# A tensor-product message kernel on one core: the product of the gathered rows gets a tile of its own

## The chip, the cores and the metric

The kernel runs on one core of one Trainium2 chip. The metric is the device time of the whole launch in microseconds (us). Five engines have instruction streams of their own: TensorE (PE), VectorE (DVE), ScalarE (ACT), GpSimd (POOL) and SyncE (SP). They wait for one another through semaphores. In the profile, "PE" is the matmul stream and "PEld" the loading of matmul weights; a "q" behind an engine's name (PEldq, DVEq) is its sequencer, which executes waits as small instructions of their own.

## The reference

There are N = 10,000 nodes with a feature block of 64 channels x 4 components (256 float32, 1 KB a row), and E = 640,000 edges, each with a source, a destination, four harmonics and four edge features.

```python
R   = silu(edge_feat @ w_rad)                        # (E, 64)
xs  = x[src]                                         # (E, 64, 4)
tp  = einsum('eci,ef,ifo->eco', xs, Y, cg)           # (E, 64, 4)
msg = R[:, :, None] * tp
agg = segment_sum(msg.reshape(-1, 256), dst, N).reshape(N, 64, 4)
out = einsum('ncm,cd->ndm', agg, w_mix)
```

So for each edge a row of x is gathered by its source, multiplied by a radial factor per channel, multiplied with the four harmonics, and summed into its destination node. The kernel sums x[src] * R * Y per destination first and applies `cg` and `w_mix` together to the sums (`wf` in the code).

## The kernel before

**Sort and messages.** The edges come in no order, so the kernel sorts them by destination in two passes (`pass1`, `pass2`), and the sorted edges then go through `messages()`. The edge list is cut into three parts (`SPLIT`, 32%, 37% and 31% of the edges), so that the sort of a later part runs while the messages of an earlier one are computed. The first 0.7 ms are sort alone; from then to about 10.06 ms the work of messages and the work of sort stand side by side on every engine; a short tail takes the few edges that did not fit.

**Units.** `messages()` goes through 939 units, 313 for each part. A unit is one block of 32 destination nodes, with its edges in tiles of 128: 5 tiles a unit in the first part (stage 1 here, 0.74 to 3.71 ms), 6 tiles in the second (stage 2, 3.72 to 7.03 ms). In the third (stage 3, 7.04 to 10.06 ms) units go in pairs: the even one has 6 tiles, the odd one 5, and the last tile of the even one may hold edges of both, so the odd unit's sums read it too. There are 156 such shared tiles. Stages 2 and 3 add to running sums that the stage before left in HBM (`old`, fetched by SP).

**What a unit does**, with the lines of the profile:
- gather (POOL, L1028): one indirect DMA for each tile fetches 128 rows of x into the unit's tile `xg`, [128, 6, 256] float32, of which there are `LG + 2` = 7 buffers.
- turn (PE, L1041), turned (ACT, L1046), radial (PE, L1053/1054), silu (ACT, L1057): the radial factors R of the unit come into `pre` in PSUM.
- spots (DVE, L1064, L1067): S, which says per edge which of the 32 nodes it goes to, times its harmonics. For a shared tile L1072 and L1074 make a second one, `Sx`, for the odd unit.
- products (DVE, L1081): R times the gathered rows, written over them: `xg` is operand and output. For a shared tile, `VX` keeps the view of it for the next unit's sums.
- sums (PE, L1094): per tile two matmuls of the product with S (in the trace each shows as two records), added up in `G`, one PSUM tile of which the even and the odd units take one half each. An odd unit with a shared tile has two more (`Sx`).
- evict (ACT, L1119, in stage 1; DVE, L1117, after that): G goes to `Gp` (stages 1 and 2, written back to HBM by SP, L1121) or `Gs` (stage 3). Every fourth unit of stage 3 the 128 nodes in `Gs` are multiplied with `wf` (PE, L1136) and stored.

**The order.** PE, DVE and ACT execute in the order in which the program is written (a manual schedule); what they do for other units is laid out by offsets in `quarters`: in step k the program writes, in four quarters with pieces of the sort between them,

```python
((index, LI), (gather, LG), (fetch, 2), (turn, 2), (sums, 0), (silu, 1), ...),
((turned, 2), (spots, 1)),
((products, 1), (evict, -1), ...), ((radial, 2), (full, -1))
```

The number is how many units ahead of k the piece works. So DVE does the product of unit k+1 and right behind it, in the same quarter, the eviction of unit k-1; the sums of unit k stand two quarters earlier in the program. Since both halves of `G` are one tile, the eviction of unit k-1 waits until the sums of unit k have been written. POOL and SP are not in the manual schedule: the order of their DMAs is chosen by a scheduler when the kernel is built, and waits follow from which buffer is free.

Of the kernel before, what the change touches and what calls it, by code (L numbers as in the profile page):

```python
# [18 lines left out]
F = mybir.dt.float32  # L19
BF = mybir.dt.bfloat16  # L20
I32 = mybir.dt.int32
OP = mybir.AluOpType
# [3 lines left out]
P = 128  # L26
# [10 lines left out]
PT = 2 * BT - 1  # L37
UT = 6
SPLIT = ((0.32, 5), (0.37, 6), (0.31, 6))
LG = 5  # L40
LI = 8
HEAVY = 4
BIG = 16384.0
# [36 lines left out]
class Kernel:  # L80
# [853 lines left out]
    def messages(self):  # L934

        nc, ph = self.nc, self.ph
# [3 lines left out]
        IDX, XG, PRE, ST_, RT, SS, VS, GP, GS, OLD, E9, ER, SX, VX = ({} for _ in range(14))  # L940
# [14 lines left out]
        def tiles(k):  # L955
            return place(*units[k])

        def shared(k):

            g, j = units[k]  # L960
            return g[0] == FIN and j % 2 == 0 and j + 1 < self.nb(g[1])
# [36 lines left out]
        def piece(q):  # L998
            def cast(k):

                at = block(k)
                if at is None:
                    return
                key, v, n = at
                if q == 0:
                    E9[key] = ph.tile([P, HB * MT, 3, 3, 4], BF, name="e9", bufs=2)
                    ER[key] = ph.tile([P, HB * MT, 4], F, name="er", bufs=1)
                r = ER[key][:, :n] if q else v
                nc.scalar.activation(E9[key][:, :n, :, q, :], r.unsqueeze(2).to_broadcast([P, n, 3, 4]), AF.Copy)
            return cast  # L1010
# [11 lines left out]
        def gather(k):  # L1022
            g, j = units[k]
            si, (t0, ut) = IDX[g][0], tiles(k)
            xg = XG[k] = ph.tile([P, UT, 256], F, name="xg", bufs=LG + 2)
            for t in range(ut):
                u = t0 + t
                nc.gpsimd.indirect_dma_start(  # L1028
                    out=xg[:, t, :], out_offset=None, in_=self.x,
                    in_offset=bass.IndirectOffsetOnAxis(ap=si[:, u:u + 1], axis=0))  # L1030
# [45 lines left out]

        def products(k):
            ut = tiles(k)[1]
            V = VS[k] = XG.pop(k)[:, :ut].rearrange("p t (c i) -> p t c i", i=4)
            R = RT.pop(k).rearrange("p (t c) -> p t c", c=64)  # L1080
            nc.vector.tensor_tensor(V, V, R.unsqueeze(3).to_broadcast([P, ut, 64, 4]), op=OP.mult)  # L1081
            if shared(k):
                VX[k + 1] = V[:, ut - 1]

        def sums(k):
            ut = tiles(k)[1]
            G = GP[units[k]] = Gb[:, k % 2]
            V, S = VS.pop(k), SS.pop(k)
            terms = [(V[:, t], S[:, t]) for t in range(ut)]
            if k in VX:  # L1090
# [49 lines left out]
        def mixed(k, po):  # L1140
# [5 lines left out]
        Gb = self.ps.tile([P, 2, 2, NB, 4], F, name="G", tag="G", bufs=1)  # L1146

        quarters = (((index, LI), (gather, LG), (fetch, 2), (turn, 2), (sums, 0), (silu, 1), (piece(0), 5), (piece(1), 4),
                     (piece(2), 3)), ((turned, 2), (spots, 1)),
                    ((products, 1), (evict, -1), (rest(0), 5), (rest(1), 4)), ((radial, 2), (full, -1)))  # L1150
        todo, po = [], None
        for k in range(-LI, n + 3):
# [434 lines left out]
```

## Time and profile before

| | |
|---|---|
| time, three runs | 10113.3, 10104.97, 10112.53 us; median 10112.53 |
| the profiled execution | 10113.46 us, its span 10111.7 us, mean granted PE clock 0.798 |
| busy share of the span | PE 65%, PEld 52%, DVE 71%, ACT 45%, POOL 58% |
| the 16 DMA engines | queue 0, which holds the gathers: 732.64 MB, 25.6% of their time; queue 1: 10.0% |
| gathers | 5165 indirect DMAs, POOL busy 955 ns for each |
| products | 939 instructions, 1516.9 us busy |
| sums | 20,660 records, 3256.9 us busy, and 624 for `Sx`, 125.7 us |

No engine is busy for the whole span. A row of the groups reads: line, engine, operation, output<-input, shapes, count | busy us and mean ns of one | idle time of the engine just before these instructions and what ended most of it. "issue" is time in which the engine waited for nothing that the profile shows, and "remote" is a release that the profile can't tie to an instruction of this core's records. Matmul ends are modelled.

### The profile page before, as it was taken

What the parts mean: (1) busy time and instruction counts of PE and PEld (TensorE: products, weight loads), DVE (VectorE), ACT (ScalarE), POOL (GpSimd) and SP (SyncE); (2) the same over time, 40 slices, a digit from 0 to 9 for tenths busy, and PEclk for the clock granted to TensorE, in tenths of its full rate; (3) what the DMA queues carried; (4) which work ended last, traced back from release to release, by engine and by line L of the source; (5) the groups of instructions that cost most, each with busy time, mean ns of one, the idle gap of its engine ahead of it and who ended that gap; (6) DMA issues with size and microseconds to landing.
All of it is one profiled execution on the core that took longest, in us unless ns stands there. A gap on an engine that the chain in (4) does not pass through costs nothing. (4 is left out here: it accounts for less than half of the span.)

```text
span 10111.7 us, 128908 instructions
## 1 busy us (share of the span) xinstructions
PE 6552.8 (65%) x41164; PEld 5274.4 (52%) x41164; DVE 7218.1 (71%) x15096; ACT 4528.0 (45%) x12427; POOL 5874.3 (58%) x6113
## 2 busy tenths in 40 slices
PE   5656666666666566666666666666667676666666
PEld 3335555555555455455555455555555555555555
DVE  8977878788876777777777777667565665656554
ACT  6865656555655454444444445333232333323221
POOL 1236666656666566666666566666556555565655
PEclk8867878887777777777877787777787888787888
DMA  5213333333333333333334333344333333333332
GB/s 177 103 46 107 97 102 97 104 95 103 98 100 98 100 104 113 108 114 112 111 110 117 106 108 110 112 120 117 100 95 106 94 103 99 96 105 94 105 94 80
DMA packets 696490, 1051.26 MB, mean 104 GB/s; under 512 B 273797, under 2 KB 504115, under 8 KB 695800
## 3 DMA queue, kind: packets, MB, share of 16 engines
q0 software_dynamic: 285888, 732.64, 25.6%
q1 hardware_dynamic: 407320, 301.10, 10.0%
q10 hardware_dynamic: 2592, 9.19, 0.2%
q8 instruction: 327, 5.36, 0.2%
q14 instruction: 363, 2.97, 0.1%
HBM read 841.86 MB, written 215.89 MB: 105 GB/s over the span
## 5 line engine op out<-in xcount | busy, mean ns | idle before, releaser
L1028 POOL DMA_INDIRECT xg<-in_x_dram,sidx x5165 | 4933.9, 955 | 3087.1 <-issue 1331.2
L1094 PE MATMUL G<-S,xg 128*128 128x128 f32 x20660 | 3256.9, 324 | 748.8 <-issue 319.2
L1094 PEld LDWEIGHTS G<-S,xg 128*128 128x128 f32 x20660 | 3073.1, 236 | 815.1 <-issue 350.2
L673 PE MATMUL pr<-X,oh 128*128 128x300 bf16 (+1 forms) x10573 | 1855.6, 329 | 840.0 <-DVE oh L657 328.2
L665 ACT ACTIVATE sq<-i,rowf 128x128 f32<-128x128 f32 x6132 | 1881.9, 391 | 10.5 <-DVE rowf L626 7.4
L641 DVE TENSOR_TENSOR X<-dv,Wt 128x1800 f32<-128x1800 f32 (+4 forms) x906 | 1741.8, 1923 | 202.4 <-remote 112.1
L673 PEld LDWEIGHTS <-oh 128*128 128x128 bf16 x10573 | 1127.2, 110 | 1426.0 <-issue 534.7
L1081 DVE TENSOR_TENSOR xg<-xg,pre 128x1536 f32<-128x1536 f32 (+1 forms) x939 | 1516.9, 1615 | 495.9 <-ACT pre L1057 307.8
L1057 ACT ACTIVATE pre<-pre 128x384 f32<-128x384 f32 (+1 forms) x939 | 425.7, 453 | 1639.8 <-remote 862.0
L666 ACT ACTIVATE oh<-sq,ones 128x1024 bf16<-128x1024 f32 (+3 forms) x906 | 967.1, 1067 | 31.4 <-remote 4.1
L1067 DVE TENSOR_TENSOR S<-dv,pay 128x768 f32<-128x768 f32 (+1 forms) x939 | 836.7, 891 | 133.9 <-remote 64.7
L681 ACT ACTIVATE rt<-pr 128x300 bf16<-128x300 f32 (+1 forms) x906 | 360.3, 398 | 1132.4 <-remote 703.4
L1117 DVE TENSOR_TENSOR Gs<-old,G 128x256 f32<-128x256 f32 x313 | 131.1, 419 | 940.5 <-remote 522.8
L685 POOL DMA_INDIRECT bkt<-rt,idx x489 | 493.8, 1010 | 501.7 <-ACT rt L681 137.6
L685 POOL DMA_INDIRECT grp<-rt,idx x417 | 418.3, 1003 | 595.3 <-ACT rt L681 269.2
L1041 PEld LDWEIGHTS <-e 128*108 128x108 bf16 x1878 | 245.3, 149 | 823.4 <-issue 632.0
L1041 PE MATMUL pre<-identb,e 128*108 128x128 bf16 x1878 | 304.9, 249 | 562.2 <-DVE xg L1081 418.5
L1046 ACT ACTIVATE sT<-pre 108x256 bf16<-108x256 f32 x939 | 354.0, 377 | 567.3 <-PE pre L1041 271.9
L1136 PE MATMUL po<-wf,Gs 128*128 128x256 f32 (+2 forms) x1392 | 408.4, 458 | 199.7 <-DVE Gs L1117 113.6
L1053 PE MATMUL pre<-wr,sT 108*128 108x192 bf16 x939 | 253.4, 270 | 355.9 <-ACT sT L1046 257.4
L1117 DVE TENSOR_TENSOR Gp<-old,G 128x256 f32<-128x256 f32 x313 | 130.7, 417 | 494.3 <-remote 341.9
L1136 PEld LDWEIGHTS po<-wf,Gs 128*128 128x128 f32 (+2 forms) x1392 | 302.9, 224 | 294.5 <-DVE Gs L1117 113.7
(288 smaller groups left out, 6509.0 us busy)
## 6 DMA issues: line engine op xcount, KB each, us to landing
xg<-in_x_dram,sidx POOLq DMA_INDIRECT x5165
sums<-Gp SPq DMA_DIRECT2D x626, 128.0 KB
old<-sums SPq DMA_DIRECT2D x626, 128.0 KB
bkt<-z SPq DMA_DIRECT2D x26, 990.0 KB
pay<-bkt SPq DMA_DIRECT2D x68, 225.0 KB
grp<-z SPq DMA_DIRECT2D x17, 590.0 KB
Wt<-grp SPq DMA_DIRECT2D x17, 590.0 KB
ye<-in_Y_dram SPq DMA_DIRECT2D x103, 96.0 KB
```

What stands on the lines that cost most here:

```text
L641: nc.vector.tensor_tensor(X[:, :m, :].rearrange("p t (s w) -> p t s w", w=W), msk.unsqueeze(3).to_broadcast([P, m, ps.r, W]), QD[c // Q][1 ...
L665: nc.scalar.activation(sq[:, u, :], self.i128, AF.Square, bias=to, scale=-1.0)
L666: nc.scalar.activation(oh[:, v:v + len(at), :], sq[:, :len(at), :], AF.Relu, bias=self.ones[:, 0:1], scale=-2.0)
L673: nc.tensor.matmul(pr[:, :2 * ps.rw], oh[:, u, :], X[:, u, :].bitcast(BF), start=(u == 0), stop=(not on and u == m - 1))
L685: st = nc.gpsimd.indirect_dma_start(out=ps.dst, out_offset=bass.IndirectOffsetOnAxis(ap=idx[:, i:i + 1], axis=0), in_=RT.pop(c), in_offset ...
L1028: nc.gpsimd.indirect_dma_start(out=xg[:, t, :], out_offset=None, in_=self.x, in_offset=bass.IndirectOffsetOnAxis(ap=si[:, u:u + 1], axis=0))
L1041: nc.tensor.matmul(pre[:KR, 256 + 128 * h:384 + 128 * h], e[:, 36 * t:36 * t + KR], self.identb, start=True, stop=True)
L1057: nc.scalar.activation(RT[k], RT[k], AF.Silu)
L1067: nc.vector.tensor_tensor(S[:, :ut], self.eq[:, :ut].unsqueeze(3).to_broadcast([P, ut, NB, 4]), pb[:, :, 1:5].unsqueeze(2).to_broadcast([P ...
L1081: nc.vector.tensor_tensor(V, V, R.unsqueeze(3).to_broadcast([P, ut, 64, 4]), op=OP.mult)
L1094: nc.tensor.matmul(G[:, h].rearrange("p n f -> p (n f)"), v[:, 32 * h:32 * h + 32, :].rearrange("p c i -> p (c i)"), s.rearrange("p n f -> ...
L1136: nc.tensor.matmul(po[:nn, :256], Gs[:, h, f].rearrange("p b n -> p (b n)")[:, :nn], self.wf[:, h, f, :], start=(h + f == 0), stop=(h + f ...
```

## The change

The product no longer goes over the gathered rows. It is written to a new tile `V` of the same shape, which has the pool's default of two buffers, and the sums read `V`. The tile of gathered rows has five buffers instead of seven (`LG + 1` with `LG` = 4), so the same number of bytes is held (7 tiles before, 5 + 2 now), and the gather stands four units ahead of the sums in the program instead of five.

```diff
-LG = 5
+LG = 4
@@ def gather(k)
-            xg = XG[k] = ph.tile([P, UT, 256], F, name="xg", bufs=LG + 2)
+            xg = XG[k] = ph.tile([P, UT, 256], F, name="xg", bufs=LG + 1)
@@ def products(k)
-            V = VS[k] = XG.pop(k)[:, :ut].rearrange("p t (c i) -> p t c i", i=4)
+            x = XG.pop(k)[:, :ut].rearrange("p t (c i) -> p t c i", i=4)
+            V = VS[k] = ph.tile([P, UT, 64, 4], F, name="V")[:, :ut]
             R = RT.pop(k).rearrange("p (t c) -> p t c", c=64)
-            nc.vector.tensor_tensor(V, V, R.unsqueeze(3).to_broadcast([P, ut, 64, 4]), op=OP.mult)
+            nc.vector.tensor_tensor(V, x, R.unsqueeze(3).to_broadcast([P, ut, 64, 4]), op=OP.mult)
             if shared(k):
                 VX[k + 1] = V[:, ut - 1]
```

From the product on, lines move down by one (L1081 is now L1082, the sums L1095, the evictions L1118 and L1120). On PE, DVE and ACT the instructions stand in the same order as before; what differs is what they wait for. The lists below are the program's, with the semaphores for which each instruction waits: `DMASW0` to `DMASW7` are those of POOL's DMAs (the gathers are spread over the eight), `DMAHW` of SP's, the others of engines.

PE, at the sums of an odd unit of stage 3 with a shared tile. Before, the first matmul of each tile waits for that tile's gather:

```order
L1041 MATMUL pre<-identb,e_63354 108x128 [waits PE_49]
L1041 LDWEIGHTS e_63354
L1041 MATMUL pre<-identb,e_63354 108x128
L1094 MATMUL G<-S,xg 128x128 [waits DMASW1_49]
L1094 MATMUL G<-S,xg 128x128
L1094 MATMUL G<-S,xg 128x128 [waits DMASW2_49]
L1094 MATMUL G<-S,xg 128x128
L1094 MATMUL G<-S,xg 128x128 [waits DMASW3_49]
```

Now:

```order
L1041 MATMUL pre<-identb,e_63980 108x128 [waits PE_49]
L1041 LDWEIGHTS e_63980
L1041 MATMUL pre<-identb,e_63980 108x128
L1095 MATMUL G<-S,V 128x128 x10
L1095 MATMUL G<-Sx,V 128x128 x2
```

The sums wait for no DMA any more; the first of a unit still waits for DVE where the order does not already imply it.

DVE, at the product of an even unit of stage 3 with a shared tile, before:

```order
L1064 TENSOR_TENSOR dv<-dv,dlc 128x192 [waits DVE_49]
L1067 TENSOR_TENSOR S<-dv,pay 128x768 [waits DVE_49]
L1072 TENSOR_SCALAR eqx<-dv,dlc 128x32
L1074 TENSOR_TENSOR Sx<-eqx,pay 128x128 [waits DVE_49]
L1081 TENSOR_TENSOR xg<-xg,pre 128x1536 [waits DMASW5_49,DMASW4_49,DMASW6_49,DMASW1_49,DMASW7_49,DMASW0_49,Activation_49]
L1117 TENSOR_TENSOR Gs<-old,G 128x8x32 [waits DMAHW4_49,PE_49]
```

Now:

```order
L1064 TENSOR_TENSOR dv<-dv,dlc 128x192 [waits DVE_49]
L1067 TENSOR_TENSOR S<-dv,pay 128x768 [waits DVE_49]
L1072 TENSOR_SCALAR eqx<-dv,dlc 128x32
L1074 TENSOR_TENSOR Sx<-eqx,pay 128x128 [waits DVE_49]
L1082 TENSOR_TENSOR V<-xg,pre 128x1536 [waits DMASW2_49,DMASW3_49,DMASW1_49,DMASW6_49,DMASW0_49,DMASW7_49,PE_49,Activation_49]
L1118 TENSOR_TENSOR Gs<-old,G 128x8x32 [waits DMAHW4_49,PE_49]
```

The product of unit k+2 waits for PE as well: the buffer of `V` that it writes was last read by the sums of unit k+1, which read the shared tile of unit k. 154 units have this. In all other units the buffer's reader is the sums of the unit itself, which are further back.

POOL, at the first gathers of a unit. Before, the buffer was last read by the sums:

```order
L1028 DMA xg<-in_x_dram,sidx 128x256 [waits DMASW1_49,DVE_49,PE_49]
L1028 DMA xg<-in_x_dram,sidx 128x256 [waits DMASW2_49]
L1028 DMA xg<-in_x_dram,sidx 128x256 [waits DMASW3_49]
L1028 DMA xg<-in_x_dram,sidx 128x256 [waits DMASW4_49]
L1028 DMA xg<-in_x_dram,sidx 128x256 [waits DMASW5_49]
```

Now by the product:

```order
L1028 DMA xg<-in_x_dram,sidx 128x256 [waits DMASW1_49,DVE_49]
L1028 DMA xg<-in_x_dram,sidx 128x256 [waits DMASW2_49]
L1028 DMA xg<-in_x_dram,sidx 128x256 [waits DMASW3_49]
L1028 DMA xg<-in_x_dram,sidx 128x256 [waits DMASW4_49]
L1028 DMA xg<-in_x_dram,sidx 128x256 [waits DMASW5_49]
```

A gather's first wait is for the product of five units before it, where it was for the sums of seven units before. Since the scheduler sees the gathers four units ahead and no longer five, the sort's stores on POOL (L685) stand earlier among them: by some 8 gathers on average for the `bkt` stores and some 6 for the `grp` stores.

## The prediction

> **What bounds the kernel now.** I read the busy rows and the clock first, then the windows by stage, then the waits of stage 3, where the change does most.
>
> ```profile
> PE 6552.8 (65%) x41164; PEld 5274.4 (52%) x41164; DVE 7218.1 (71%) x15096; ACT 4528.0 (45%) x12427; POOL 5874.3 (58%) x6113
> ...
> PEclk8867878887777777777877787777787888787888
> ...
> L1028 POOL DMA_INDIRECT xg<-in_x_dram,sidx x5165 | 4933.9, 955 | 3087.1 <-issue 1331.2
> L1094 PE MATMUL G<-S,xg 128*128 128x128 f32 x20660 | 3256.9, 324 | 748.8 <-issue 319.2
> ...
> L1081 DVE TENSOR_TENSOR xg<-xg,pre 128x1536 f32<-128x1536 f32 (+1 forms) x939 | 1516.9, 1615 | 495.9 <-ACT pre L1057 307.8
> L1117 DVE TENSOR_TENSOR Gs<-old,G 128x256 f32<-128x256 f32 x313 | 131.1, 419 | 940.5 <-remote 522.8
> ```
>
> No engine is full. The gathers are the costliest group, but 3087 of POOL's 4237 us of idle time lie in front of them, and what ends DVE's wait in front of the products is ACT, not a gather. The windows by stage (length; busy us of PE, PEld, DVE, ACT, POOL; clock, DMA share, GB/s):
>
> ```profile
> 1000.00:3700.00 2700.00, 1782.50 (x11580) 1427.40 (x11581) 2149.81 (x4519) 1518.16 (x4250) 1653.94 (x1713) 0.80 0.34 99
> 3750.00:7000.00 3250.00, 2049.59 (x13065) 1669.08 (x13064) 2360.28 (x4602) 1424.57 (x3834) 2031.37 (x2116) 0.78 0.39 112
> 7080.00:10050.00 2970.00, 2018.71 (x12316) 1701.51 (x12316) 1741.89 (x3535) 867.69 (x2396) 1742.88 (x1815) 0.81 0.35 99
> ```
>
> In stages 1 and 2 DVE is busiest (80% and 73%); in stage 3 PE is (68%), and DVE has 59%. There the two hand work to each other, as the waits of that stage show (who waited <- for whom: us, times, longest):
>
> ```profile
> DVE Gs L1117 <- remote: 518.4, 90, 12.9
> POOL xg L1028 <- PE G L1094: 383.6, 77, 12.3
> DVE Gs L1117 <- PE G L1094: 229.9, 66, 9.0
> PEld G L1094 <- DVE Gs L1117: 126.2, 66, 7.7
> DVE xg L1081 <- ACT pre L1057: 115.6, 28, 8.9
> PE G L1094 <- DVE Gs L1117: 114.9, 33, 7.6
> PE pre L1041 <- DVE xg L1081: 58.8, 35, 7.4
> ```
>
> DVE stands at the evictions for 518 + 230 = 748 us, a quarter of the stage, until PE's sums are done, and PE stands before sums for some 115 to 126 us until an eviction is done. So stage 3 runs by the loop sums, eviction, next sums, with PE's other work between. POOL's 384 us of waiting for sums is the wait that the change takes away.
>
> **The change part by part.** The base is the profiled execution, 10113.5 us (0.9 above the median of the three runs; span 10111.7, 1.8 around it).
>
> *The gathers.* Their buffer is released by the product of five units before, no longer by the sums of seven units before. That takes away the 384 us of POOL's wait in stage 3, but POOL has to be on a path for this to count. A gather costs:
>
> ```profile
> 8004.16 0.95 POOL L1028 DMA_INDIRECT xg<-in_x_dram,sidx  x1 [0.30 <-issue]
> ```
>
> 1.25 us with its issue; 1815 POOL instructions of stage 3 by that are 2269 of 2970 us (76%), so POOL keeps up. How far ahead it is, the windows of `xg` alone show (busy and count of PE, PEld, DVE, POOL up to four times):
>
> ```profile
> 0.00:3000.00 3000.00, 755.99 (x4740) 713.74 (x4740) 352.79 (x238) 1168.40 (x1220) 0.81 0.35 103
> 0.00:5000.00 5000.00, 1451.26 (x9116) 1370.27 (x9116) 673.13 (x433) 2210.07 (x2314) 0.80 0.36 104
> 0.00:8000.00 8000.00, 2559.95 (x16118) 2412.90 (x16119) 1171.16 (x725) 3827.29 (x4009) 0.79 0.37 106
> 0.00:9000.00 9000.00, 2940.49 (x18548) 2767.72 (x18548) 1333.90 (x826) 4359.44 (x4567) 0.80 0.36 105
> ```
>
> At 3000 us 238 products have used 238 x 5 = 1190 tiles and 1220 are gathered: 30 tiles ahead, 6 units. At 5000 us 313 x 5 + 120 x 6 = 2285 are used of 2314: 29 tiles, 4.8 units. At 8000 us 1565 + 1878 + 50 x 6 + 49 x 5 = 3988 of 4009: 21 tiles, 3.8 units; at 9000 us 4543 of 4567: 24 tiles. A unit takes some 9.65 us in stage 3 (3.02 ms for 313), so the least lead seen is some 37 us. With five buffers and release by the product, the gathers can be at most four whole units ahead of the product that is being made, where now they are up to five or six: I take one to one and a half units off, and some 22 to 27 us stay. A DMA's way to its landing, in the chain that ends the kernel:
>
> ```profile
> 10074.38 3.17 DMA out_dram<-ot
> ...
> 10082.42 2.58 DMA ocur<-out_dram,osm
> ```
>
> About 3 us. Cover of 22 us against 3 us: I cost the shorter lead, and the earlier stores among the gathers, at nothing. The wait removed from POOL costs nothing before and saves nothing now. If the cover were gone, DVE's products would wait, and then PE's sums behind them. The view of the product's line is the nearest price of that:
>
> ```profile
> L1081 DVEq EVENT_SEMAPHORE  x2815: 21/50/1264, 737.8 to 10059.9; - x188
> DMA xg<-in_x_dram,sidx: 84.2, 32
> ```
>
> 84 us of waiting is put down to gathers now; since the lead is units long, I read it as a wait for several semaphores of which a DMA's event happened to be the last, later gathers using the same semaphores. Bounds for this part: 0 to +84 us (twice of what is booked); I take 0.
>
> *The sums.* They lose their DMA waits. What they cost, from the view of the sums' line:
>
> ```profile
> L1094 PEldq EVENT_SEMAPHORE  x782: 51/51/51, 755.4 to 10056.6; - x196
> ```
>
> 782 x 51 ns = 40 us if every one goes and none lies beside other work. They are in the sequencer of a stream that waits before the sums anyway for an eviction or a product. Bounds -40 to 0; I take a quarter, -10.
>
> *The product.* Same operands in number, type and shape, another output; nothing in the trace separates a product over its own input from one elsewhere. The nearest row is a product of two f32 inputs into another tile, the one into `S`: 0.96 us for 768 elements a partition in the DVE rows below, 1.25 ns an element; the product takes 1.75 us for 1536, 1.14 ns, so being in place doesn't show as a penalty that could be saved. 0. The extra wait on PE in 154 units is one more sequencer event of about 50 ns: 0 to +8 us; I take +3.
>
> *The shared tile.* This is what the change adds. In stage 3 the product of an even unit k+2 must now wait for the sums of unit k+1, which read the shared tile of unit k from the same buffer. Behind it on DVE is the eviction of unit k, which waits for these very sums already. One such place, DVE and then PE:
>
> ```profile
> 8003.13 0.96 DVE L1067 TENSOR_TENSOR S<-dv,pay 128x768 f32<-128x768 f32 x1
> ...
> 8004.59 1.75 DVE L1081 TENSOR_TENSOR xg<-xg,pre 128x1536 f32<-128x1536 f32 x1
> 8011.31 0.42 DVE L1117 TENSOR_TENSOR Gs<-old,G 128x256 f32<-128x256 f32 x1 [4.97 <-PE G L1094]
> ```
>
> ```profile
> 8010.24 0.39 PE L1094 MATMUL G<-Sx,xg 128*128 128x128 f32 x2 [0.31 <-issue]
> 8011.71 0.34 PE L1053 MATMUL pre<-wr,sT 108*128 108x192 bf16 x1 [1.08 <-ACT sT L1046]
> ...
> 8012.91 0.42 PE L1041 MATMUL pre<-identb,e 128*108 128x128 bf16 x2
> 8013.12 2.23 PE L1094 MATMUL G<-S,xg 128*128 128x128 f32 x9
> ```
>
> The product ran at 8004.59, in time in which DVE had nothing else, and the eviction then waited 4.97 us, to 8011.31, for sums whose last record ends at 8010.63. Now the product begins at about 8011.31: 6.7 us later, but all behind it only by its own length, 1.75 us. The eviction ends at 8011.31 + 1.75 + 0.42 = 8013.48. What is late next is PE: its next sums, of unit k+2, need this eviction and this product. They began at 8013.12; PE had radial, turn and sort work up to there. So they slip 0.36 us, and the turn at 8012.91, which needs the `pre` buffer that the product frees at 8013.06, slips 0.15; it is the wait that has 58.8 us in 35 places now. The price of a shared unit is thus 0 where PE has work for 2.2 us or more behind the sums, and 1.75 us where it has none: 154 x 1.75 = 270 us at most, in a stage where DVE has 1228 us idle. All 154 like the example give 154 x 0.36 = 55 us. Evictions end a wait of PE's in 66 of the stage's units, half of them even: 33 x 0.36 = 12 us. I take +12, between 0 and 270, since in the other units something else than the eviction came last in front of the sums. In stages 1 and 2 the buffer of `V` is released by the sums of two units before, which the order of PE and DVE has finished by then; nothing is added there.
>
> *Sum:* 0 - 10 + 3 + 12 = +5, so 10113.5 + 5 = 10118 us.
>
> On the recorded ends, the eviction at 8020.14 shows how far to trust them:
>
> ```profile
> 8013.12 5.05 PE L1094 MATMUL G<-S,xg 128*128 128x128 f32 x24
> ```
>
> ```profile
> 8020.14 0.42 DVE L1117 TENSOR_TENSOR Gs<-old,G 128x256 f32<-128x256 f32 x1 [1.50 <-PE pre L1041]
> ```
>
> These sums end at 8018.17 by the records and the eviction begins 1.97 us after that, so PE can be later than it looks, and with it less of the 1.75 us may be covered. [...]
>
> **The rivals.**
>
> *B, the shared tile is paid in full (slower).* If PE really has no spare work between an odd unit's sums and the next even unit's, each of the 154 units costs between 0.36 and 1.75 us. For it: the 748 us at evictions, and the late true ends. Against: PE's idle time before sums that an eviction ends is only some 120 us. 10113.5 + 55 = 10169 us at 0.36; with half of 1.75, 135 us, 10248. It decides from about 0.13 us a unit (20 us in all).
>
> *C, PE gains (faster).* All 782 events go and none was hidden: 10113.5 - 40 = 10073 us. For it: 319.2 of PE's 748.8 us of idle time in front of the sums are booked as "issue", with no other cause. Against: the same stream then waits for DVE.
>
> *D, PE's clock falls.* The rows have a clock of 0.81 in stage 3 and 0.78 in stage 2, where nothing but the work's grain differs on PE. If the added pauses bring stage 3 to 0.78 and PE binds, 2018.7 x (0.81 / 0.78 - 1) = 78 us: 10191. Against: the pause added at the place shown is 0.36 us. [...]
>
> *E, the gathers come late (slower).* Lead lost where POOL is held by stores of the sort: +84 us by the booked wait, 10197. Against: 22 us of cover.
>
> That the change doesn't do what it says can't be in the waits, which are in the program; that POOL's freed time brings nothing is the forecast itself.
>
> **How the numbers follow.** About 0.2% (20 us) is what a measurement of this kernel can tell from no change. The forecast, absorbed, 10118 us with its own range 10095 to 10135: 0.43. B: 0.25; C: 0.20; D: 0.07; E: 0.05. B, D and E are slower, together 0.37; C is faster, 0.20; the rest within 0.2%, 0.43. The range reaches from a little below C, 10062, to 10210, which takes in B at 0.36 us, D and E, and leaves out B's upper part; outside are some 2 in 10.
>
> **What would show it.** In the profile after: no waits of the sums for gathers and almost no sequencer events at their line; the gathers wait for the product, no more for the sums, with POOL's idle time much the same; in stage 3 the new product waits for PE (several hundred us) and the evictions' 748 us shrink by about as much; the boundaries of stages 1 and 2 within 10 us of 3.71 and 7.03 ms. Wrong would be the forecast if stage 3 grows by over 20 us with PE's wait for evictions above 200 us (B), with a clock under 0.80 (D), or if products wait for gathers for more than 150 us (E); if stages 1 and 2 get shorter by over 10 us each, it is C.

## The result: 8.5% slower

The change takes 10973.95 us (median of four runs, 10949.82 to 10979.4), the kernel before 10112.12 (10104.97 to 10113.3): 1.0849 times, with a 95% interval of 1.083 to 1.0868. The forecast was 10118 with a range of 10062 to 10210. So the range was missed by 764 us, and the step that failed is not the one that the prediction held to be risky.

The profiled execution of the change is 10949.82 us, its span 10948.0, 836 us above the span before. Its page:

```profile
PE 6760.6 (62%) x41164; PEld 5441.9 (50%) x41164; DVE 7205.2 (66%) x15096; ACT 4541.1 (41%) x12427; POOL 5878.2 (54%) x6113
...
L1028 POOL DMA_INDIRECT xg<-in_x_dram,sidx x5165 | 4937.2, 956 | 2744.7 <-issue 1437.6
L1095 PE MATMUL G<-S,V 128*128 128x128 f32 x20660 | 3452.6, 336 | 1110.9 <-issue 521.0
...
L1082 DVE TENSOR_TENSOR V<-xg,pre 128x1536 f32<-128x1536 f32 (+1 forms) x939 | 1516.9, 1615 | 1290.9 <-remote 443.1
...
L1057 ACT ACTIVATE pre<-pre 128x384 f32<-128x384 f32 (+1 forms) x939 | 425.2, 453 | 2320.5 <-remote 1380.4
L685 POOL DMA_INDIRECT bkt<-rt,idx x489 | 494.0, 1010 | 1219.9 <-ACT rt L681 577.0
...
L685 POOL DMA_INDIRECT grp<-rt,idx x417 | 418.7, 1004 | 1033.8 <-ACT rt L681 585.2
```

The rows of silu and of the sort's stores in the page of before:

```profile
L1057 ACT ACTIVATE pre<-pre 128x384 f32<-128x384 f32 (+1 forms) x939 | 425.7, 453 | 1639.8 <-remote 862.0
...
L685 POOL DMA_INDIRECT bkt<-rt,idx x489 | 493.8, 1010 | 501.7 <-ACT rt L681 137.6
L685 POOL DMA_INDIRECT grp<-rt,idx x417 | 418.3, 1003 | 595.3 <-ACT rt L681 269.2
```

On DVE, ACT and POOL nothing got slower: the product has 1615 ns on average in both, the gather 956 and 955, and each of the three engines is busy for the same time within 14 us. PE is busy for 208 us more, its sums taking 336 ns on average instead of 324 (ends modelled) at a granted clock of 0.769 instead of 0.798. How much of these 208 us lies on the path, no run here tells. On POOL the loss is all waiting, and there it adds up: before its gathers it stands 2744.7 us instead of 3087.1, but before the two kinds of stores 1219.9 + 1033.8 instead of 501.7 + 595.3. Together that is 4998 instead of 4184 us, 814 of the 836.

Where in the program, the evictions tell, whose first and last starts mark the stages (the lines of the evictions; after, then before):

```profile
L1118 DVE TENSOR_TENSOR Gp<-old,G x313: 400/415/423, 4130.0 to 7817.1; 128x256 f32<-128x256 f32 x157
L1118 DVE TENSOR_TENSOR Gs<-old,G x313: 410/414/423, 7822.9 to 10906.2; 128x256 f32<-128x256 f32 x157
```

```profile
L1117 DVE TENSOR_TENSOR Gp<-old,G x313: 402/416/423, 3747.2 to 7057.5; 128x256 f32<-128x256 f32 x157
L1117 DVE TENSOR_TENSOR Gs<-old,G x313: 414/420/423, 7063.0 to 10069.7; 128x256 f32<-128x256 f32 x157
```

Stage 1 ends 383 us later, stage 2 takes 3687 us instead of 3310 (377 more), stage 3 3083 instead of 3007 (76 more). The loss is almost all in stages 1 and 2, where the prediction had the change cost nothing.

**What the trace of before had already shown.** "Remote" was, in this trace, almost always a wait on PE's semaphore (915 of 926 places). The trace records the semaphore's updates themselves, and they can be laid beside the recorded ends of the instructions that make them. DVE's and ACT's come 0.01 us after those ends (median). PE's come late, in half of the cases by some 0.2 us before and 0.02 after, in one of ten by 5.49 and 6.39, in one of a hundred by 10.65 and 14.16. The lateness goes with POOL issuing indirect DMAs one behind the other. Before, PE's updates come at some 0.6 a microsecond in the first two of such a run, at some 0.1 when it has lasted for 10 to 12, and at 2.5 to 3.3 (by how short runs are counted) in the third microsecond after it ends, when what was held comes out in a row. (In the traces below with updates in time the rate is 0.4 to 0.7 at all of these places.) One place in stage 1 of the change shows it (timeline; in brackets the wait and its releaser):

```profile
1563.68 4.00 PE L1095 MATMUL G<-S,V 128*128 128x128 f32 x20 [1.79 <-issue]
...
1574.41 0.95 POOL L1028 DMA_INDIRECT xg<-in_x_dram,sidx  x1 [0.30 <-issue]
1575.66 1.01 POOL L685 DMA_INDIRECT grp<-rt,idx  x1 [0.30 <-issue]
1579.60 0.39 ACT L1120 ACTIVATE Gp<-G 128x256 f32<-128x256 f32 x1 [10.41 <-remote]
...
1580.04 4.34 PE L1095 MATMUL G<-S,V 128*128 128x128 f32 x20 [11.52 <-ACT Gp L1120]
...
1587.82 0.39 ACT L681 ACTIVATE rt<-pr 128x280 bf16<-128x280 f32 x1
1588.10 0.43 ACT L1057 ACTIVATE pre<-pre 128x320 f32<-128x320 f32 x1
1588.48 1.00 POOL L685 DMA_INDIRECT grp<-rt,idx  x1 [11.81 <-ACT rt L681]
1588.57 1.49 DVE L1082 TENSOR_TENSOR V<-xg,pre 128x1280 f32<-128x1280 f32 x1 [0.35 <-ACT pre L1057]
1589.79 0.98 POOL L1028 DMA_INDIRECT xg<-in_x_dram,sidx  x1 [0.30 <-issue]
```

The sums end at 1567.68 by the records. POOL gathers on and stops at 1576.67 at a store; three microseconds after that, at 1579.60, the eviction may begin, ACT, DVE and PE having stood for ten. Then POOL, which is at a store of the sort, goes on standing until PE and ACT have done the next piece of sort (`rt`), to 1588.48. Between the recorded end of the sums and the start of the eviction lie 11.9 us (1567.68 to 1579.60). What fills them, the profile does not say.

This changes what the gather's wait means. In this condition PE's results come out in POOL's pauses, and whatever stands between that and POOL's next DMA is paid each time. (That the gathers hold them is argued from the coincidence in time; the held kernels below impose it.) Before, POOL pauses for over 1.5 us in front of a gather 534 times, and the gather starts 0.26 us (median) after the first PE update in the pause. After, there are 241 such pauses, 212 of them with a PE update, and the gather starts 2.6 us after it. In front of the sort's stores, such pauses go from 99 to 338.

All these pauses together, split at the first PE update in them, tell what grew. Up to that update they last 1194 us before and 993 after; from it to POOL's next DMA 816 and 1677. So POOL does not stand longer until PE's results begin to come out. It stands 861 us longer when they have begun to, 764 of it in front of stores, which wait for ACT's `rt`, and 97 in front of gathers, which wait for the product. Where POOL stops has changed: before, mostly at a gather that PE's sums release at once, now more often at a store than at a gather.

### The profile page after: what moved, and what is told of

The parts are those of the page before. It is cut to its first block, busy times and chain, and to the rows that moved or that the text cites. A ratio compares the mean times of both kernels' runs of the same rounds, so it can differ in the third digit from the quotient of the medians.

```text
span 10948.0 us, 128266 instructions
## 1 busy us (share of the span) xinstructions
PE 6760.6 (62%) x41164; PEld 5441.9 (50%) x41164; DVE 7205.2 (66%) x15096; ACT 4541.1 (41%) x12427; POOL 5878.2 (54%) x6113
## 5 line engine op out<-in xcount | busy, mean ns | idle before, releaser
L1028 POOL DMA_INDIRECT xg<-in_x_dram,sidx x5165 | 4937.2, 956 | 2744.7 <-issue 1437.6
L1095 PE MATMUL G<-S,V 128*128 128x128 f32 x20660 | 3452.6, 336 | 1110.9 <-issue 521.0
L1095 PEld LDWEIGHTS G<-S,V 128*128 128x128 f32 x20660 | 3238.4, 247 | 1221.0 <-issue 576.2
L1082 DVE TENSOR_TENSOR V<-xg,pre 128x1536 f32<-128x1536 f32 (+1 forms) x939 | 1516.9, 1615 | 1290.9 <-remote 443.1
L685 POOL DMA_INDIRECT bkt<-rt,idx x489 | 494.0, 1010 | 1219.9 <-ACT rt L681 577.0
L685 POOL DMA_INDIRECT grp<-rt,idx x417 | 418.7, 1004 | 1033.8 <-ACT rt L681 585.2
L1118 DVE TENSOR_TENSOR Gp<-old,G 128x256 f32<-128x256 f32 x313 | 130.7, 417 | 904.0 <-remote 717.7
L1137 PE MATMUL po<-wf,Gs 128*128 128x256 f32 (+2 forms) x1392 | 379.3, 434 | 135.9 <-DVE Gs L1118 100.8
L1120 ACT ACTIVATE Gp<-G 128x256 f32<-128x256 f32 x313 | 119.7, 382 | 742.4 <-remote 495.4
L657 DVE TENSOR_TENSOR oh<-dv,pair 128x640 bf16<-128x640 bf16 (+2 forms) x869 | 420.6, 488 | 2.4 <-issue 2.3
```

The source lines that it names most:

```text
L657: nc.vector.tensor_tensor(oh[:, :v, :].rearrange("p t (h k) -> p t h k", k=2), self.vb.rearrange("p (h k) -> p h k", k=2).unsqueeze(1).to_ ...
L685: st = nc.gpsimd.indirect_dma_start(out=ps.dst, out_offset=bass.IndirectOffsetOnAxis(ap=idx[:, i:i + 1], axis=0), in_=RT.pop(c), in_offset ...
L1028: nc.gpsimd.indirect_dma_start(out=xg[:, t, :], out_offset=None, in_=self.x, in_offset=bass.IndirectOffsetOnAxis(ap=si[:, u:u + 1], axis=0))
L1082: nc.vector.tensor_tensor(V, x, R.unsqueeze(3).to_broadcast([P, ut, 64, 4]), op=OP.mult)
L1095: nc.tensor.matmul(G[:, h].rearrange("p n f -> p (n f)"), v[:, 32 * h:32 * h + 32, :].rearrange("p c i -> p (c i)"), s.rearrange("p n f -> ...
```

## The experiments

The theories, by the names used in the expectations: **runs of gathers** (a release by the product lets POOL's runs get longer, and PE's results stay held for longer; the split of the pauses above already speaks against it), **short lead** (five buffers are too few), **store order** (the sort's stores stand earlier among the gathers), **V's two buffers** (the product waits for the sums that read V), and, formed later, **the product stands in the chain** (the gather's buffer, once freed by the sums, is now freed by the product, which stands behind PE and ACT). The kernel before took 8,411 to 8,425 us in most of the following measurements, and 10,090 in two. In the first kind PE's updates are in time (0.02 us in 99 of 100) in every trace taken beside it, held kernels included; in the second they are late as above. Each comparison is against before measured beside it.

### Parts of the change

The product in place, with the five buffers and the gather four units ahead:

```diff
-LG = 5
+LG = 4
-            xg = XG[k] = ph.tile([P, UT, 256], F, name="xg", bufs=LG + 2)
+            xg = XG[k] = ph.tile([P, UT, 256], F, name="xg", bufs=LG + 1)
```

> The product is written over the gathered rows again, as before; the five buffers and the gather four units ahead stay as in the change. Theory 'runs of gathers' (PE's releases come late while POOL issues gathers without a pause, and a release of the gather's buffer by the product instead of the sums lets these runs get longer): the sums release the buffers again, so 10,050 to 10,250 us, with the longest run of gathers back at about 15. Theory 'short lead' (five buffers are too few, products wait for gathers): released even later than in the change, so 10,950 us or more. Theory 'store order' (the sort's stores stand earlier among the gathers and hold them up): the stores stand 10 gathers (bkt) and 7 (grp) earlier than before, so 10,950 or more. Theory 'V's two buffers' (products wait for the sums that read V): no V, so 10,080 to 10,150.

The change with the gather five units ahead (`LG = 5`, `bufs=LG`):

> The change, but with the gather five units ahead in the program as before (five buffers, V with two). The stores stand as in the change. All four theories: 10,900 to 11,050, unless it is the place of the gather in the program, four units ahead instead of five, that costs the time: then 10,080 to 10,250.

The kernel before with the gather four ahead (`LG = 4`, `bufs=LG + 3`):

> The kernel before with the gather four units ahead instead of five and still seven buffers, the product in place. The stores stand as before among the gathers. All four theories: 10,080 to 10,150. If the place of the gather itself costs: 10,900 or more.

The change with three buffers for V and four for the gathered rows:

> The change with three buffers for V and four for the gathered rows (the same bytes). The stores stand among the gathers as before. Theory 'runs of gathers': a run may take four units at most, not five, so better than the change: 10,300 to 10,750. Theory 'short lead': one buffer less, 11,300 or more. Theory 'store order': 10,080 to 10,200. Theory 'V's two buffers': the product has a buffer more, no shared wait: 10,080 to 10,200.

All four met PE's updates in time: 8416.91, 8408.54, 8407.42 and 8427.92 us, against 8412.24; the ratios are 1.0006 (0.9997 to 1.0016), 0.9997 (0.9988 to 1.0007), 0.9995 (0.9985 to 1.0004) and 1.0019 (1.0009 to 1.0029). Every theory's number was missed, since none had foreseen that before itself would be 17% faster. In one point the last expectation is wrong: in its kernel the stores stand not as before but earlier by 14 gathers (bkt) and 9 (grp), more than in the change. So the change and five buffers in place were measured beside each other:

> The change itself, once more. On the chip of the four runs just before, PE's semaphore updates came at most 0.02 us after the recorded ends (99 in 100), the kernel before took 8412 us, and all four variants 8407 to 8428. If the 8.5% belong to a chip on which PE's releases come late (10 in 100 by 5.5 us or more in the first profile), then this run is at 8400 to 8440 us where before takes some 8412, and at 10,900 to 11,050 where before takes some 10,110. If they belong to the kernel alone: 1.08 times before in either case.

> Five buffers released by the sums, product in place. Where before takes some 8412 us: 8410 to 8425 again. Where before takes some 10,110: theory 'runs of gathers' 10,050 to 10,250; theory 'short lead' or 'store order' 10,950 or more; theory 'V's two buffers' 10,080 to 10,150.

8410.72 us and 0.9997 (0.9987 to 1.0006) for the change, 8416.93 and 1.0007 (0.9997 to 1.0017) for the other. With PE's updates in time the change costs nothing that can be measured. The page of the change there:

```profile
PE 6021.2 (72%) x41164; PEld 4989.8 (59%) x41164; DVE 7192.4 (86%) x15096; ACT 4536.9 (54%) x12427; POOL 5873.9 (70%) x6113
...
L1028 POOL DMA_INDIRECT xg<-in_x_dram,sidx x5165 | 4932.8, 955 | 1705.0 <-issue 1358.0
...
L1082 DVE TENSOR_TENSOR V<-xg,pre 128x1536 f32<-128x1536 f32 (+1 forms) x939 | 1516.9, 1615 | 727.2 <-DMA xg<-in_x_dram,sidx 477.7
```

1358.0 of the 1705.0 us in front of the gathers are the 0.3 us of issue: POOL hardly pauses, and products wait 478 us for gathers. POOL is near the bound here (5165 + 906 indirect DMAs at 1.25 us are 7.6 of the 8.4 ms), and what frees a buffer does not matter, since buffers are free when POOL comes to them.

### PE held on purpose

To have the late condition at will, PE's release was tied to the gathers: ahead of the last tile's matmuls of a unit's sums stands one that reads the last gathered tile of a later unit, the furthest whose gather may run: six ahead in before and in the change, four ahead with five buffers in place. In all of them silu and products were put ahead of the gather and the sums in a step, which the hold needs:

```diff
-        quarters = (((index, LI), (gather, LG), (fetch, 2), (turn, 2), (sums, 0), (silu, 1), ...
+        quarters = (((index, LI), (silu, 1), (products, 1), (gather, LG), (fetch, 2), (turn, 2), (sums, 0), ...
@@ def gather(k)
+            HELD[k] = xg[:, ut - 1, :128]
@@ def sums(k)
+            hold = HELD.get(k + LG)
             for t, (v, s) in enumerate(terms):
+                if hold is not None and t == len(terms) - 1:
+                    nc.tensor.matmul(G[:, 0].rearrange("p n f -> p (n f)")[:, :1], hold, self.zero,
+                                     start=False, stop=False, skip_group_check=True)
```

> The kernel before with PE's release held on purpose: ahead of the last tile's matmuls of a unit's sums stands a matmul that reads the last gathered tile of the unit six ahead (times a zero, added to G) and so waits for its landing; the gather stands six units ahead, and in a step silu and products stand ahead of gather and sums. This imitates, on any chip, what the first profiles show: sums that are released only when the gathers that may run have landed. The loop is then sums, six gathers and a store on POOL, their landing, sums: 8.1 us of POOL, 2.5 to 3 of landing and some 1 of matmuls, 10.5 to 12.5 us a unit, 10,500 to 12,500 us in all, under every theory.

> The change with the same hold and the same order (V with two buffers, five for the gathered rows, gather six units ahead, released by the product of five before). Theory 'the product stands in the chain': the seventh unit's gather ahead is freed by the sums in both kernels, but here by way of V and the product, so each unit costs a product and its wait more, 0.9 to 1.8 us, 850 to 1,700 us in all: 1.07 to 1.15 times held_before. Theory 'runs of gathers' without the product in a chain: within 3% of held_before, since the hold is the same. Theory 'short lead' (five buffers): slower than held_before as well, and so is held_inplace_five.

> Five buffers, product in place, the gather and the hold four units ahead, same order of the step. Theory 'the product stands in the chain': the sums release the gather directly, so within 3% of held_before. Theory 'short lead': like held_after or slower.

11798.85 us for before with the hold, 16606.3 for the change with it, 11788.94 for five buffers in place: the change is 1.407 times before under the same hold (16606.3 / 11798.85), five buffers with the product in place 0.999. The sign and the parting of the theories are as the chain has it, the size is three to six times the 850 to 1,700 us expected. POOL's rows (held before, held after, held five in place):

```profile
L1032 POOL DMA_INDIRECT xg<-in_x_dram,sidx x5165 | 4923.3, 953 | 4673.8 <-PE G L1102 2698.2 <-issue 1278.5 <-PE pre L1058 493.9
L687 POOL DMA_INDIRECT bkt<-rt,idx x489 | 493.1, 1008 | 666.2 <-ACT rt L683 318.8 <-ACT ot L1151 149.8 <-issue 92.6
L687 POOL DMA_INDIRECT grp<-rt,idx x417 | 417.7, 1002 | 542.3 <-ACT rt L683 227.7 <-issue 75.2 <-DMA grp<-z 61.6
```

```profile
L1032 POOL DMA_INDIRECT xg<-in_x_dram,sidx x5165 | 4926.2, 954 | 6847.7 <-DVE dv L1068 3149.1 <-DVE V L1086 1500.4 <-issue 1332.2
L687 POOL DMA_INDIRECT bkt<-rt,idx x489 | 495.7, 1014 | 2370.6 <-ACT rt L683 1624.0 <-ACT ot L1152 180.2 <-ACT sT L1050 129.5
L687 POOL DMA_INDIRECT grp<-rt,idx x417 | 417.8, 1002 | 1438.4 <-ACT rt L683 943.6 <-DMA grp<-z 68.3 <-issue 63.9
```

```profile
L687 POOL DMA_INDIRECT bkt<-rt,idx x489 | 494.0, 1010 | 650.2 <-ACT rt L683 328.5 <-ACT ot L1151 133.5 <-issue 94.8
```

It is the signature of the change: POOL's waits for PE's sums become waits for DVE (put down to `dv` where that stands right behind the product; POOL goes on 0.27 us after the product's end in these places, as it does after the sums before), and the stores, which stand behind, wait 3.6 and 2.7 times as long. In the held five in place the stores stand earlier among the gathers than in any other held kernel, by 11 gathers (bkt) and 8 (grp) against before, and they wait no longer (650.2 and 545.3 us). That speaks against the store order, and the time against the short lead.

Why so large? The product of unit k+2 needs V from the sums of unit k, but also R, and R's matmuls stand behind the sums of unit k in PE's order, with ACT's silu behind them. Three buffers for V, four for the gathered rows and gather and hold five ahead part the two:

> held_after with three buffers for V and four for the gathered rows, gather and hold five units ahead, so that the product of unit k+1 waits for the sums of k-2 and no longer of k-1. Theory 'V's two buffers' (the product stands still until the sums give V back): the loop now spans two units, so 11,000 to 12,500 us, near held_before (11,799). Theory 'the product's operands' (the product also needs R, whose matmuls stand behind the held sums on PE, and ACT's silu behind them, so that sums, radial, silu, product and gather are one chain however many V there are): 15,500 to 17,000, as held_after (16,606).

15822.59 us: of the 4807 us between the held kernels, 784 go and the rest stays. This kernel also has a buffer less for the gathered rows, a hold one unit nearer and stores earlier by 10 and 7 gathers, so the 784 are not V's third buffer alone. But no product in it stands behind PE's sums any more (556.0 us did in the held change), and they wait for ACT's silu for 2425.5 us. So in this imitation it is mainly the product's operands. Then the hold on every second unit only (`if k % 2 == 0`):

> held_before with the hold on every second unit only, nearer to the first profiles, where a part of the releases is late. Every theory: between 8,412 and 10,100 us (half of held_before's loss), less than that where the other unit makes up for it.

> held_after with the hold on every second unit only. Theory 'the product stands in the chain': 1.05 to 1.25 times held_even_before, the loss growing with the share of held units. If the chain mattered only with every unit held: within 2% of held_even_before.

10343.33 and 12773.83 us, 1.235 times; the first is slightly above its range, the second at the upper end of its. The loss grows with the share of held releases, and the size first measured lies where before, at 10,112 us, is a little less held than this. That is an ordering, not a calibration: how the late releases are spread over the units differs from the imitation.

### POOL's part where the updates are in time

SP copies the last tile of each unit in POOL's place:

```diff
+            nc.sync.dma_start(xg[:, ut - 1, :], self.x[:P, :])
-            for t in range(ut):
+            for t in range(ut - 1):
```

> The kernel before, but the last tile of each unit is not gathered by POOL: SP copies the first 128 rows of x there with a plain DMA (so the last tile's messages are not those of its edges); the bytes are the same, POOL has 939 instructions less. If POOL's issue of the gathers bounds the kernel where it takes 8412 us (5165 + 906 indirect DMAs at 1.25 us are 7.6 ms of it): 939 x 1.25 = 1174 us less, 7,150 to 7,500 us. If POOL is not on the path, as the prediction says: 8,350 us or more.

7932.35 us against 8411.89, 0.9426 times (0.9411 to 0.9442): 480 us, neither none nor 1174. The engine row suggests why it stops there:

```profile
PE 5888.5 (74%) x41164; PEld 4878.6 (61%) x41164; DVE 7187.9 (91%) x15096; ACT 4529.1 (57%) x12427; POOL 4984.7 (63%) x5174
```

DVE is at 91% of the span. POOL's part of the gathers was on the path, with DVE close behind it. (The rows of the last tile also come in one plain DMA of another queue here; that part of the gain was not measured by itself.)

### Where the releases are late again

> held_after without the hold: the same order of the step, five buffers, gather six units ahead, V with two buffers. If the hold, and not the order of silu, product and gather in the step, makes held_after slow: 8,380 to 8,700 where before takes some 8,412. If the order does: 10,000 or more.

> The change on whatever chip this is. Where PE's releases are in time: within 0.3% of before. Where they come late: 1.07 to 1.10 times before.

Here before took 10089.25 us, with PE's updates late as in the first trace (median 0.02, one of ten by 6.41, one of a hundred by 14.04 us in the change). The change took 10957.72, 1.0864 times (1.0838 to 1.089), and held_after without its hold 10940.33, 1.0851 (1.0832 to 1.0871). With late updates, the order of the step and the gather six ahead or four make no difference. The numbers expected for the order were written for before at 8,412, so "10,000 or more" is met here without saying anything for it; where updates are in time, the order alone was not run. The 8.5% came back. Then the run that decides:

> Five buffers released by the sums, product in place, the gather four units ahead; the sort's stores stand 2 gathers earlier still than in the change. Where before takes some 8,412 us: equal to it. Where before takes some 10,100 us (late releases): theory 'the product's operands stand in the gather's chain' 9,950 to 10,300; theories 'short lead' and 'store order' 10,850 or more.

10088.8 us against 10089.99, 0.9996 times (0.9983 to 1.0008), with late updates again (0.17, 5.47 and 10.28 us):

```profile
L1028 POOL DMA_INDIRECT xg<-in_x_dram,sidx x5165 | 4945.5, 957 | 3087.1 <-issue 1335.4
...
L685 POOL DMA_INDIRECT bkt<-rt,idx x489 | 493.2, 1009 | 491.8 <-issue 126.2
...
L685 POOL DMA_INDIRECT grp<-rt,idx x417 | 418.6, 1004 | 584.4 <-ACT rt L681 256.3
```

Everything of the change is in this kernel but V: five buffers, gather four ahead, stores earlier by 11 and 7 gathers. POOL's waits are those of before to within 11 us. So short lead and store order are out, and the whole loss belongs to the product's own tile, that is, to a gather that is freed by the product and a product that writes elsewhere. (The product's own tile beside seven buffers of gathered rows was not run.) The split of POOL's pauses says the same: 1161 us up to the first PE update and 829 from it here, as before; 990 and 1673 in the change beside it. What of the loss is V's two buffers was to be told by three of them:

> The change with three buffers for V and four for the gathered rows; the stores stand as in the kernel before. Where before takes some 8,412 us: 1.000 to 1.003 times. Where it takes some 10,100 (late releases): theory 'V's two buffers' 10,050 to 10,300; theory 'the product's operands' (the buffer of the gathered rows hangs on the product, which stands behind radial on PE and silu on ACT, however many V there are) 10,750 to 11,200.

> The same kernel again, for a chip with late releases: theory 'V's two buffers' 10,050 to 10,300 us, theory 'the product's operands' 10,750 to 11,200, where before takes some 10,100. Where before takes some 8,412: 1.002 times.

Both met updates in time, 8427.75 and 8427.37 us, 1.0019 (1.0009 to 1.0028) and 1.0017 (1.0007 to 1.0027). So under late releases a third buffer was not measured. The first trace of the change tells where it could matter, by what the products wait for (windows of stage 1 and of stage 2, the longest row of each):

```profile
DVE V L1082 <- ACT pre L1057: 102.0, 44, 7.1
```

```profile
DVE V L1082 <- ACT pre L1057: 56.2, 16, 14.7
```

In these two stages no product's wait is put down to PE's sums or to "remote"; all 443.1 + 135.9 us of these lie in stage 3. So in the stages that lose 760 of the 836 us a buffer of V is free by the time the product's other operands are there, and the loss there is the gather's release.

## Why the prediction was wrong

**The gathers.** This is the step that failed, a wait put at nothing: "The wait removed from POOL costs nothing before and saves nothing now", "I cost the shorter lead, and the earlier stores among the gathers, at nothing". The arithmetic of the lead was right as far as it went, and five buffers in place do lose nothing. The window of `xg` in the change (length; busy and count of DVE and POOL, clock, DMA) still has 1075 - 210 x 5 = 25 tiles of lead:

```profile
0.00:3000.00 3000.00, 311.20 (x210) 1030.81 (x1075) 0.77 0.31 93
```
But a lead answers whether rows are there in time. It does not answer who starts POOL again after each pause, and here that decided, since PE's results came out in POOL's pauses. Freed by the sums, POOL goes on at once (0.26 us). Freed by the product, it goes on after PE's radial, ACT's silu and DVE's product as well (2.6 us). More often it is no longer stopped at a gather but runs on to a store, which blocks it until ACT's `rt`, behind the same late evictions. Measured: +814 us of POOL's waiting, where the sum had 0.

**The shared tile.** Here the mechanism was right and the size too small: stage 3, on which the prediction spent its care, lost 76 us, between the 12 that it took and the 270 of its bound. Products wait for PE (435.3 us in 60 places put down to "remote") and the evictions for less (127.4 + 76.5 us in the line's view instead of 748). What is paid is the prediction's own second item, the turn that needs the buffer `pre` which the late product frees: 354.2 us in 115 places instead of 58.8 in 35.

```profile
DVE V L1082 <- remote: 435.3, 60, 10.6
...
PE pre L1041 <- DVE V L1082: 354.2, 115, 9.6
```

"In stages 1 and 2 the buffer of V is released by the sums of two units before, which the order of PE and DVE has finished by then; nothing is added there" holds for V's buffer, as the rows above show; what those stages lose is the gather's term. The prediction had also seen an eviction start 1.97 us after the recorded end of its sums, and drew from it only that "less of the 1.75 us may be covered".

**The sums** lost their sequencer events, as foreseen: no such row is left in the view of their line. A gain of 10 to 40 us is not to be seen under the loss. **The product** costs the same, 1615 ns on average, as foreseen.

**The rivals.** B had the sign, but with its place in stage 3, and its own mark is missing: there PE's waits before sums for an eviction fell from some 115 to 10 us. C is refuted where it could have shown: with PE's updates in time the change is at 0.9997. D: the clock did fall, from 0.798 to 0.769, while PE's idle time in front of the sums went from 748.8 to 1110.9 us. In the held runs the two go together as well (0.763 in before with 3611.8 us of waits at the hold, 0.684 in the change with 8226.9), and where the change costs no time it does not fall (0.857, before 0.850). E had the sign and the place, POOL held up by stores, with too small a price (84 us) and a chance of 0.05; its sign in the profile, products waiting for gathers for more than 150 us, was there (215.1), though five buffers in place, whose gathers are released later still, lose nothing; so these waits go with the loss and do not make it. The mistake behind them all is one of reading. 518 us of "remote" in front of evictions, the largest wait of stage 3, were put down to PE's sums, and the prediction did not ask why the profile could not tie them to these sums.

## What to carry to other kernels

A wait that is never the last one by the lead may still be the one that paces a loop. Before moving the release of a buffer from one engine to another, list what stands between the two releases (here radial, silu, product), and where the waiting engine will stop instead (here at the sort's stores), and ask what it costs if the first of them is late. A wait whose releaser the profile does not name deserves a cause before any term is set to nothing, and the semaphore updates laid beside the recorded ends can give it.

## What was not expected of the hardware

The same program had two speeds that differ by 20%: before at 8,411 to 8,425 us and at 10,089 to 10,112, and on one of the chips both, at different times (8425.26 and 10089.99 us). In the slower, PE's semaphore updates come late while POOL issues indirect DMAs (in the first trace of before one of ten by 5.49 us); in the faster, 99 of 100 come within 0.02 us, though POOL then runs almost without a pause (in after_again 1358.0 of the 1705.0 us in front of its gathers are the 0.3 us of issue). In the slower the traces also lack records: in the first trace of before, of DVE's 12,453 updates 8,039 are there, of PE's 4,780 4,295; in the faster, with seven buffers and the gather four ahead, 12,438 and 4,769. Whether what holds PE's updates is also what loses the records, and whether the recording itself has a part in it, stays open: no run here was made without it.
